# Convolution and a 16-expert layer on one core: narrower channel rows, ids alone in the token lists, and no GpSimd product

## The chip, the cores and the metric

The kernel runs on one core of a Trainium2 chip. The metric is the device time of one execution in microseconds (us). The kernel before takes 1279.42 us, the median of three runs (1278.69 to 1280.14). The engines are named as in the profile: PE (TensorE, matmuls and transposes), PEld (its weight loads), DVE (VectorE), ACT (ScalarE), POOL (GpSimd) and SP (SyncE, which issues most of the loads).

## The reference, cut to what matters

```python
# x: 8 x 2880 x 192; weight: 8 heads x 7 taps; N = 23040 tokens, D = 192, 4 x 4 experts, F = 1024
w = softmax(weight, axis=-1)
x = causal_conv(x, w)                  # per head of 24 channels, 7 taps, zeros ahead of each sequence
g_sm = softmax(x @ w_group);           g_idx = argmax(x @ w_group)
e_sm = softmax(x @ w_expert[g_idx]);   e_idx = argmax(x @ w_expert[g_idx])
out  = g_sm[g_idx] * e_sm[e_idx] * (relu(x @ w1[g_idx, e_idx]) @ w2[g_idx, e_idx])
```

Each token is sent to one expert of 16, and its result is scaled by the product of the two probabilities, its weight.

## The kernel before, in words

**Routing.** Tokens are handled in blocks of 120. A unit is a group of blocks: three units of 4, 8 and 12, three of 8, 8 and 8, then 12 each, 18 units (u0 to u17) in all. For each unit the input `xin` is loaded by SP; for each of 8 heads one matmul with a banded matrix makes the convolution (L419), and ACT copies it from PSUM into the unit's channel tile `xc` (L428). Rows of `xc` have XW = 256 columns: the 192 channels stand in columns 64 to 255, and ACT copies the last 64 of them once more into columns 0 to 63 (L431). ACT then issues the write of the whole tile to `xcd` in DRAM (L436), where the experts' stage finds a token's row by its id. `xc` rotates over 2 buffers (the pool `pa2`), so unit u+2's first copy needs unit u's write to be over.

Router logits need more than one pass of precision: the tile is transposed (L446, and L462 or L470) and split into a rounded part and a rest (ACT L449, L465, L471; DVE L450, L466, L472). From u8 on the last 64 channels of two blocks are transposed together, 128 columns at once (L462, "packed"); this needs two split steps on ACT and on DVE. Earlier units transpose block by block (L470). Three matmuls (L483) and transposes back (L495) give the logits; DVE and ACT make softmax and argmax (L531 to L562).

**Lists.** A unit's tokens get a position in the list of their expert. DVE writes two one-hot tables for six blocks at a time: `ohl` (L608) and `ohr` (L612, one buffer). POOL multiplies `ohr` by five bf16 columns `vals` (the low and high part of the id, and the weight in three bf16 pieces, L562 to L565) into `lts` (L616), and one matmul per block adds these up in PSUM (L631, 5 x 32 = 160 columns). ACT copies the result out (L637), DVE puts ids and weights together (L638 to L643), and POOL scatters them into the table `idtab` in DRAM, two columns (L645).

**Experts.** The work is a plan of slots of 256 tokens. Portion 0 has one slot for each of 16 experts and starts once u0 to u4 are listed; portion 1 has two per expert (needs u0 to u11) and portion 2 two more (needs all 18); the tail, nine items of 256 and nine of 128 tokens, is laid out at run time by DVE (`table`) from the counts. For a slot POOL gathers rows from `xcd` (L711, two gathers, into `xg` with 3 buffers), PE transposes them (L724, L726, or packed, L724 and L728, in portions 1 and 2), ACT and DVE split them (L729 to L741), and PE runs the first layer (`ph`, L752), whose output ACT (L757) and DVE (L758) turn into `hh` and `hl`, and then the second (`po`, L770 and L774). `finish` scales by the weight, read from the second column of the ids (ACT L821, DVE L822, tile `ys`), and POOL scatters the rows to the output (L825). Small tail items go through L787 to L813. An expert's weights come in five loads on SP (L660 to L664) into `raw` (6 buffers, a set needs 4) and are split by ACT and DVE (L676 to L692; in the tail POOL takes one of the splits, L685).

**What sets the order.** Each engine works through its own list in order. A generator per unit is stepped (`step`), and during the slots `advance` steps it between blocks of matmuls at a rate that has the units ready in time for the next portion; a tile scheduler then orders each engine's list by priorities. So list and routing steps of u5 to u17 lie between the matmuls of portions 0 and 1, while in portion 2 only expert work is left.

**The end.** Two loops stand behind the plan, each with a trip count read at run time: one (L1198) rebuilds the lists if an expert's share of one unit is too large, one (L1237) takes tail items beyond the 18. With these inputs both run zero times.

## Time and profile before

| | us |
|---|---|
| median of 3 runs | 1279.42 |
| the profiled execution | 1276.92 |
| its span, first to last instruction | 1275.2 |
| PE busy | 1132.9 (89%) |
| DVE busy | 907.9 (71%) |
| ACT busy | 721.9 (57%) |
| POOL busy | 554.1 (43%) |

The profiled execution stands 2.5 us under the median of the runs. PE's busy time counts matmuls only; the difference of it to the span, 142 us, is time in which PE ran none. The mean granted clock of PE is 0.941. Stages by the clock of the trace, from the span's start: until 155 us routing alone, 155 to 350 portion 0 with routing, 350 to 740 portion 1 with routing, 740 to 1101 portion 2, from 1101 the tail, whose last matmul ends at 1254.

### The profile page before, as it was taken

The page shows a single profiled execution, that of the slowest core. Times are in us where ns is not written, and L with a number is a line of the kernel's source. Part 1 is how long each engine was busy: PE and PEld are TensorE (multiplying, and loading weights), DVE is VectorE, ACT ScalarE, POOL GpSimd, SP SyncE. Part 2 cuts the span into 40 slices and gives each one's busy share as a digit, 9 for nine tenths or more (in the row PEclk, how much of TensorE's full clock was granted, in tenths as well). Part 3 has the DMA queues.
Part 4 walks back from the last instruction along what each step waited for, and adds up shares of the span by engine and source line. Part 5 has one row for each costly group of instructions (what it writes and reads, how often), then busy time and mean ns, then how long its engine had stood idle before and what let it go on. Part 6 is the DMA issues. An engine that isn't in the chain of part 4 may idle for free.

```text
span 1275.2 us, 23501 instructions
## 1 busy us (share of the span) xinstructions
PE 1132.9 (89%) x8080; PEld 1079.8 (85%) x8080; DVE 907.9 (71%) x2053; ACT 721.9 (57%) x1474; POOL 554.1 (43%) x473
## 2 busy tenths in 40 slices
PE   4677588888979999899989899999999999989993
PEld 3555487878979989898989899999999999988893
DVE  4777588898878767778677766666666665677771
ACT  4544256566756656455555355555555555677771
POOL 2121534333443443434444534444444444666751
PEclk8878688899989999899989989999999999999997
DMA  8955435777887747354454456454454544588860
GB/s 191 285 161 169 127 98 173 209 214 194 222 217 186 223 109 211 91 174 113 123 146 114 101 105 181 142 154 137 143 147 134 150 137 140 160 238 249 244 194 11
DMA packets 171740, 207.71 MB, mean 163 GB/s; under 512 B 27095, under 2 KB 145739, under 8 KB 171614
## 3 DMA queue, kind: packets, MB, share of 16 engines
q1 hardware_dynamic: 129566, 140.62, 41.0%
q0 software_dynamic: 18720, 41.93, 11.2%
q10 hardware_dynamic: 23328, 23.60, 6.0%
q8 instruction: 64, 1.05, 0.4%
q14 instruction: 62, 0.51, 0.1%
HBM read 164.92 MB, written 42.78 MB: 163 GB/s over the span
## 4 chain that ended last, share of the span: by engine, by line
PE 55%; DVE 16%; DMA 10%; issue 8%; ACT 5%; POOL 4%; SPq 1%; POOLq 0%; ACTq 0%; DVEq 0%
PE ph L752 23%; PE po L770 15%; PE po L774 7%; DMA raw<-in_moe_w 4%; POOL lts L616 3%; PE pm L419 3%; DVE hl L758 3%; DVE cw L692 2%; DMA out<-ys,idpt 2%; ACT cw L691 2%; PE pm L483 1%; PE pm L631 1%; ACT ys L821 1%; DVE tb L466 1%; DMA xcd<-xc 1%
## 5 line engine op out<-in xcount | busy, mean ns | idle before, releaser
L770 PE MATMUL po<-cw,hh 128*128 128x384 f32 x1424 | 450.7, 373 | 24.9 <-DVE ys L822 23.9
L752 PE MATMUL ph<-xa,ah 128*128 128x256 f32 x1424 | 393.6, 298 | 5.5 <-DVE hl L758 5.5
L774 PE MATMUL po<-cw,hl 128*128 128x192 f32 x1424 | 360.3, 253 | 0.0
L758 DVE SCALAR_TENSOR_TENSOR hl<-ph,hh 128x512 fp32r<-128x512 f32 x356 | 241.7, 686 | 130.2 <-ACT hh L757 124.6
L711 POOL DMA_INDIRECT xg<-xcd,idp x160 | 168.9, 1056 | 357.4 <-PE pm L728 214.2
L757 ACT ACTIVATE hh<-ph 128x512 fp32r<-128x512 f32 x356 | 209.1, 596 | 180.3 <-PE ph L752 173.7
L770 PEld LDWEIGHTS po<-cw,hh 128*128 128x128 f32 x1424 | 272.9, 192 | 30.8 <-DVE ys L822 26.8
L752 PEld LDWEIGHTS ph<-xa,ah 128*128 128x128 f32 x1424 | 276.2, 194 | 9.1 <-DVE hl L758 6.1
L774 PEld LDWEIGHTS po<-cw,hl 128*128 128x128 f32 x1424 | 276.9, 194 | 2.1
L825 POOL DMA_INDIRECT out<-ys,idp x160 | 187.2, 1170 | 120.7 <-DVE ys L822 82.3
L752 PE MATMUL ph<-xb,bh 128*128 128x256 f32 x712 | 204.4, 287 | 0.0
L752 PE MATMUL ph<-xb,bl 128*128 128x256 f32 x712 | 204.2, 287 | 0.0
L752 PE MATMUL ph<-xa,al 128*128 128x256 f32 x712 | 203.9, 286 | 0.0
L692 DVE TENSOR_TENSOR cw<-raw,cw 128x768 fp32r<-128x768 f32 x132 | 132.7, 1032 | 13.9 <-ACT cw L691 12.7
L752 PEld LDWEIGHTS ph<-xa,al 128*128 128x128 f32 x712 | 139.1, 195 | 1.8
L752 PEld LDWEIGHTS ph<-xb,bl 128*128 128x128 f32 x712 | 139.5, 196 | 0.0
L752 PEld LDWEIGHTS ph<-xb,bh 128*128 128x128 f32 x712 | 138.7, 195 | 0.0
L677 DVE TENSOR_TENSOR al<-raw,ah 128x1024 fp32r<-128x1024 f32 x66 | 82.8, 1255 | 36.3 <-ACT ah L676 23.5
L616 POOL TENSOR_TENSOR lts<-ohr,vals 120x960 bf16<-120x960 bf16 (+2 forms) x35 | 66.3, 1893 | 97.2 <-DVE ohr L612 49.3
L691 ACT ACTIVATE cw<-raw 128x768 fp32r<-128x768 f32 x132 | 105.4, 841 | 0.1
L736 ACT ACTIVATE xb<-pm 64x128 fp32r<-64x128 f32 x128 | 34.7, 271 | 92.3 <-DVE xa L730 44.2
L676 ACT ACTIVATE ah<-raw 128x1024 fp32r<-128x1024 f32 x66 | 70.0, 1060 | 27.8 <-DMA raw<-in_moe_w 11.8
(252 smaller groups left out, 1688.8 us busy)
## 6 DMA issues: line engine op xcount, KB each, us to landing
raw<-in_moe_w SPq DMA_DIRECT2D x132, 384.0 KB
raw<-in_moe_w SPq DMA_DIRECT2D x66, 512.0 KB
raw<-in_moe_w SPq DMA_DIRECT2D x132, 256.0 KB
xcd<-xc ACTq DMA_DIRECT2D x13, 1440.0 KB
xin<-in_x SPq DMA_DIRECT2D x7, 1134.0 KB
xin<-in_x SPq DMA_DIRECT2D x6, 1039.5 KB
xcd<-xc ACTq DMA_DIRECT2D x4, 960.0 KB
xg<-xcd,idp POOLq DMA_INDIRECT x160
```

Of the source, the lines that this page charges most:

```text
L616: OHE.tensor_tensor(out=ohv5[0:Q, 0:n], in0=ohr[0:Q, 0:n].unsqueeze(2).broadcast_to([Q, n, NV, LH]), in1=bc(vu[0:Q, bs], LH), op=ALU.mult,)
L676: pin(PINA, nc.scalar.activation(out=ah, in_=ra, func=AF.Copy))
L677: eng.get(k, nc.vector).tensor_tensor(out=al, in0=ra, in1=ah.bitcast(F32), op=ALU.subtract)
L691: pin(PINW, nc.scalar.activation(out=cw[:, fs, 0, :], in_=rc[k - 2], func=AF.Copy))
L692: eng.get(k, nc.vector).tensor_tensor(out=cw[:, fs, 1, :], in0=rc[k - 2], in1=cw[:, fs, 0, :].bitcast(F32), op=ALU.subtract,)
L711: nc.gpsimd.indirect_dma_start(out=xs[:, t, :], out_offset=None, in_=xcd[0:known, :], in_offset=bass.IndirectOffsetOnAxis(ap=ids[:, t, 0:1 ...
L752: nc.tensor.matmul(out=hp[:, j], lhsT=wgt[:, fs], rhs=xx, start=i == 0, stop=i == len(ops) - 1)
L757: nc.scalar.activation(out=hh, in_=hp, func=AF.Relu)
L758: nc.vector.scalar_tensor_tensor(out=hl, in0=hp, scalar=0.0, in1=hh.bitcast(F32), op0=ALU.max, op1=ALU.subtract,)
L770: nc.tensor.matmul(out=oo[t][:, 0:2 * D], lhsT=hh[:, j, ts], rhs=cw[:, f].rearrange("p a d -> p (a d)"), start=f == 0, stop=False,)
L774: nc.tensor.matmul(out=oo[t][:, 0:D], lhsT=hl[:, j, ts], rhs=cw[:, f, 0, :], start=False, stop=f == NF - 1,)
L825: nc.gpsimd.indirect_dma_start(out=outviews[nscat[0] % len(outviews)], out_offset=bass.IndirectOffsetOnAxis(ap=ids[:, t, 0:1].bitcast(U32) ...
```

## The change

- Rows of `xc`, `xcd` and `xg` have 193 columns (XW = D + 1): 192 channels, then the token's weight. The copy into the doubled columns (L431) goes. `reciprocal` writes the weight straight into column 192 of `xc`, and the write to `xcd` moves behind it, from the end of the convolution to the end of the softmax; it is still issued by ACT, the whole unit at once. `xc` gets a third buffer.
- `vals` has two columns (the id). The five DVE steps on the weight (L562 to L565) and two on the lists (L642, L643) go. The product with `ohr` moves from POOL to DVE, has a tile `ohv` of its own, and makes 6 x 2 x 32 = 384 columns instead of 960; the list matmul has 64 columns instead of 160. `idtab` has one column.
- Packed transposes go, in the router (from u8 on two more transposes per quarter unit of four blocks, one split step less on ACT and on DVE) and in the slots of portions 1 and 2 (four transposes instead of three, one split step less on ACT and on DVE).
- `finish` reads the weight from the gathered row. `xg` gets a fourth buffer.
- Weights: `raw` and `rawc`, three buffers each, instead of six `raw`; in the tail the loads of a set are issued up to three slots further ahead, every second set into `xin` and `xc` tiles, which are free by then.
- The two loops at the end are nested in an outer loop, whose flag the table's code works out, so that one loop is skipped instead of two. `LISTLAG0` is 0 and changes nothing.

The core of the diff:

```diff
-NV = 5
+NV = 2
-    RAWB = 6
+    RAWB = 3
-    XW = D + D2
+    XW = D + 1
-    idtab = dram.tile([ROWS, 2], I32, name="idtab")
+    idtab = dram.tile([ROWS, 1], I32, name="idtab")
-    OHE = nc.gpsimd
+    OHE = nc.vector
-    NXG = 3
+    NXG = 4
...
-        xc = pa2.tile([P, UB, XW], F32, name="xc")
+        xc = pa2.tile([P, UB, XW], F32, name="xc", bufs=3)
...
-            dup.tensor_copy(out=xc[0:BT, 0:nb, 0:D2], in_=xc[0:BT, 0:nb, D:XW])
-        xcw = xcd[t0:t0 + nb * BT, :].rearrange("(b p) d -> p b d", p=BT)
-        for q in range(0, nb, SQ):
-            SE.dma_start(out=xcw[:, q:q + min(SQ, nb - q)], in_=xc[0:BT, q:q + min(SQ, nb - q)])
...
-            if PACKU[0] <= u < PACKU[1]:
...
             for i in range(QB):
-                nc.tensor.transpose(psb[0:D2, i * BT:(i + 1) * BT], xc[0:BT, q * QB + i, D:XW], ident[0:BT, 0:BT])
+                nc.tensor.transpose(psb[0:D2, i * BT:(i + 1) * BT], xc[0:BT, q * QB + i, P:D], ident[0:BT, 0:BT])
...
-        nc.vector.reciprocal(out=se, in_=se)
-        nc.vector.tensor_copy(out=vu[0:Q, :, 2], in_=se)
-        for k in (3, 4):
-            nc.vector.tensor_tensor(out=se, in0=se, in1=vu[0:Q, :, k - 1], op=ALU.subtract)
-            nc.vector.tensor_copy(out=vu[0:Q, :, k], in_=se)
+        nc.vector.reciprocal(out=xc[0:Q, 0:nb, D], in_=se)
+        xcw = xcd[t0:t0 + nb * BT, :].rearrange("(b p) d -> p b d", p=BT)
+        SE.dma_start(out=xcw, in_=xc[0:BT, 0:nb])
...
-            ohv5 = pa.tile([P, 512], F32, name="lts", bufs=2).bitcast(BF16)[:, 0:HB2 * NV * LH].rearrange(
-                "p (b v r) -> p b v r", b=HB2, v=NV)
+            ohv5 = pa.tile([P, HB2, NV, LH], BF16, name="ohv", bufs=2)
...
-        nc.vector.tensor_tensor(out=lv5[:, 2], in0=lv5[:, 2], in1=lv5[:, 3], op=ALU.add)
-        nc.vector.tensor_tensor(out=lsi.bitcast(F32)[:, :, 1], in0=lv5[:, 2], in1=lv5[:, 4], op=ALU.add)
...
+        if spare:
+            rab = pa2.tile([P, UB, D], F32, name="xin").rearrange("p b d -> p (b d)")
+            ra, rb = (rab[:, k * F:(k + 1) * F] for k in range(2))
+            rcc = pa2.tile([P, UB, XW], F32, name="xc", bufs=3).rearrange("p b d -> p (b d)")
...
+            nc.tensor.transpose(px[:, t * P:(t + 1) * P], xs[:, t, 0:P], ident)
+            nc.tensor.transpose(px[0:D2, SLOT + t * P:SLOT + (t + 1) * P], xs[:, t, P:D], ident)
...
-            g = ids.bitcast(F32)[:, t, 1:2]
+            g = xs[:, t, D:XW]
...
+    def tail_weights(i, take=True):
+        if tail0 <= i < len(plan) and i not in tailw:
+            j = plan[i][1]
+            tailw[i] = weights(
+                *tail_regs(lambda c: tab[0][0:1, j, c:c + 1], 2), {1: nc.gpsimd}, spare=(i - tail0) % 2 == 0)
+        return tailw[i] if take else None
...
+        for q in range(i + 1, i + 1 + TAHEAD):
+            if tab[0] is not None and len(units) == routed[1]:
+                tail_weights(q, False)
...
-    with tc.For_i(0, nover, 1):
+    with tc.For_i(0, nrare[0], 1):
...
+        with tc.For_i(0, nover, 1):
...
+        with tc.For_i(NTAIL, nend[0], 1) as i:
```

How the order of each engine's list moves is shown at three places. The first is ACT's list in the routing stage, before, where the tile of a unit with 8 blocks is written (L436); `tb` is a split step, and the wait names in brackets are the semaphores of DMA queues (DMAHW) and engines.

```order
79 L431 ACTIVATE xc<-xc 120x8x64 [waits Activation_49]
80 L436 DMA xcd<-xc 120x8x256 [waits DMAHW3_49,Activation_49]
81 L471 ACTIVATE tb<-po 64x480 [waits PE_49]
82 L428 ACTIVATE xc<-ph 120x8x24 [waits DMAHW4_49,PE_49]
83 L471 ACTIVATE tb<-ph 64x480 [waits PE_49]
```

The same engine in the changed kernel, where a unit of 8 blocks is written (L536) and three rows further on the first convolution copy (L423, L428 before) into the next buffer waits on a DMA.

```order
73 L444 ACTIVATE tb<-po 64x480 [waits PE_49,Activation_49]
74 L536 DMA xcd<-xc 120x8x193 [waits DVE_49]
75 L461 ACTIVATE lts<-ph 120x480 [waits PE_49]
76 L444 ACTIVATE tb<-ph 64x480 [waits PE_49,Activation_49]
77 L423 ACTIVATE xc<-ph 120x8x24 [waits DMAHW0_49]
78 L423 ACTIVATE xc<-po 120x8x24
```

In both a copy into `xc` stands some three rows behind a write. Before, with two buffers, the write that the copy waits for is that of two units earlier; in the changed kernel, with three buffers and the write moved behind the softmax, it is that of three units earlier, and this is the write that stands just ahead of it.

The second place is DVE's list around the lists of a unit in portion 1, before (`hl` belongs to the hidden layer, `xa` and `xb` to the transposed rows of the next slot, `ys` to the output of the last one).

```order
831 L608 TENSOR_TENSOR ohl<-iop,posb 120x768
832 L612 TENSOR_TENSOR ohr<-ior,posb 120x192
833 L608 TENSOR_TENSOR ohl<-iop,posb 120x768
834 L466 TENSOR_TENSOR tb<-pm,tb 64x2x120
835 L612 TENSOR_TENSOR ohr<-ior,posb 120x192
836 L758 SCALAR_TENSOR_TENSOR hl<-ph,hh 128x512
837 L730 TENSOR_TENSOR xa<-pm,xa 128x256
838 L822 SCALAR_TENSOR_TENSOR ys<-po,idp_1167,ys 128x192
```

And in the changed kernel, with the products `ohv` (L586) on DVE:

```order
750 L578 TENSOR_TENSOR ohl<-iop,posb 120x768
751 L582 TENSOR_TENSOR ohr<-ior,posb 120x192
752 L578 TENSOR_TENSOR ohl<-iop,posb 120x768
753 L586 TENSOR_TENSOR ohv<-ohr,vals 120x384
754 L722 SCALAR_TENSOR_TENSOR hl<-ph,hh 128x512
755 L582 TENSOR_TENSOR ohr<-ior,posb 120x192
756 L701 TENSOR_TENSOR xa<-pm,xa 128x256
757 L586 TENSOR_TENSOR ohv<-ohr,vals 120x384
758 L786 SCALAR_TENSOR_TENSOR ys<-po,xg_197,ys 128x192
```

Two products have come in and a split step has left; the first `ys` still stands behind both `ohr`, and now behind both products too.

The third place is the end of ACT's list before, where the last `ys` stands behind the first loop's branch.

```order
1181 L821 ACTIVATE ys<-po,idpt 128x192 x2
1182 L798 ACTIVATE hh<-pm 128x512
1183 L1197 TENSOR_LOAD over
1184 L1198 COMPARE_AND_BRANCH
1185 L1198 UNCONDITIONAL_BRANCH x2
1186 L1274 BRANCH_PREFETCH_HINT
1187 L1198 REGISTER_ALU
1188 L1198 COMPARE_AND_BRANCH
1189 L1198 UNCONDITIONAL_BRANCH
1190 L821 ACTIVATE ys<-po,idpt 128x192
```

In the changed kernel the last `ys` (L785) stands ahead of the one outer branch (L1189).

```order
1121 L785 ACTIVATE ys<-po,xg_197 128x192 x2
1122 L762 ACTIVATE hh<-pm 128x512
1123 L785 ACTIVATE ys<-po,xg_198 128x192
1124 L1139 TENSOR_LOAD flagi
1125 L1189 COMPARE_AND_BRANCH
```

The last output step has moved ahead of the skip on ACT; the scatter that it feeds, on POOL, stands behind the loop in both kernels.

More of the change, by code (lines that the diff above doesn't have):

```diff
@@ L236, in conv_moe_kernel @@
     LIM = SLOT * sum(spe for _, spe in portions)
-    fill = const.tile([P, 2 * LIM // P], I32, name="fill")
+    fill = const.tile([P, LIM // P], I32, name="fill")
     nc.gpsimd.memset(fill, BIG)
@@ L445, in turn_a @@
             for i in range(QB):
-                nc.tensor.transpose(psa[:, i * BT:(i + 1) * BT], xc[0:BT, q * QB + i, D2:D], ident[0:BT, 0:BT])
+                nc.tensor.transpose(psa[:, i * BT:(i + 1) * BT], xc[0:BT, q * QB + i, 0:P], ident[0:BT, 0:BT])
             tah = pa.tile([P, QN], F32R, name="tah", bufs=QS)
@@ L625, in unit @@
         nc.vector.tensor_tensor(out=rowi, in0=rows[:, E:E + 1], in1=goff, op=ALU.add)
-        for _ in range(LISTLAG if u >= NEED else 0):
+        for _ in range(LISTLAG if u >= NEED else LISTLAG0 if u < NEED - 1 else 0):
             yield
@@ L836, in close_table @@
         yield
-        seen = const.tile([P, 2, 2], I32, name="seen")
+        seen = const.tile([P, 2, 1], I32, name="seen")
         nc.sync.dma_start(
-            out=seen, in_=TABV[0:2, :].unsqueeze(0).broadcast_to([P, 2, 2]))
+            out=seen, in_=TABV[0:2, :].unsqueeze(0).broadcast_to([P, 2, 1]))
         nc.vector.tensor_scalar(out=seen, in0=seen, scalar1=0, scalar2=BIG, op0=ALU.bitwise_and, op1=ALU.bitwise_or)
@@ L852, in close_table @@
                 yield
+    flags = const.tile([P, 2], F32, name="flags")
+    flagi = const.tile([P, 2], I32, name="flagi")
     def table(first=None, nbig=NBIG, nsmall=NSMALL):
@@ L891, in table @@
         tt(t["rem"], endr, base, ALU.subtract)
+        if first is None:
+            ts(flags[:, 0:1], most, float(SLOT), ALU.is_gt)
+            ts(flags[:, 1:2], most, float(SLOT), ALU.is_le)
+            ts(t["rem"], t["rem"], flags[:, 1:2], ALU.mult)
         slots(t["nf"], P - 1 if first is None else SLOT - 1)
@@ L934, in table @@
         v.tensor_copy(out=enti, in_=ent)
+        if first is None:
+            ts(flags[:, 1:2], ent[:, 3:4], float(NTAIL), ALU.is_gt)
+            tt(flags[:, 1:2], flags[:, 0:1], flags[:, 1:2], ALU.max)
+            v.tensor_copy(out=flagi, in_=flags)
         yield
@@ L1016, in open_tail @@
             yield
-        idps["tail"] = const.tile([P, NTAIL, 2, 2], I32, name="idpt")
+        idps["tail"] = const.tile([P, NTAIL, 2, 1], I32, name="idpt")
         for j in range(NTAIL):
@@ L1028, in open_portion @@
         rows = spe * 2
-        idp = const.tile([P, E, rows, 2], I32, name=f"idp{pi}")
+        idp = const.tile([P, E, rows, 1], I32, name=f"idp{pi}")
         if pi == 0:
@@ L1094, in open_slot @@
         if pi == "tail":
-            W = weights(*tail_regs(lambda c: tab[0][0:1, e, c:c + 1], 2), {1: nc.gpsimd})
+            W = tail_weights(i)
             ids = idps["tail"][:, e]
@@ L1162, in conv_moe_kernel, with fold @@
                 hr = hidden_small(W, turned[i], f2)
-                def fold(W=W, oo=oo, hr=hr, f2=f2, ids=ids, last=last):
+                def fold(W=W, oo=oo, hr=hr, f2=f2, ids=ids, xs=gathered[i], last=last):
                     HH = turn_small(hr)
@@ L1169, in fold2 @@
                         if last:
-                            finish(oo, ids)
+                            finish(oo, ids, xs)
                     later(LAG_S, fold2)
```

190 lines of the change are left out of this document (80 added, 110 removed).

## The prediction

> **What bounds the kernel now.** I read the page first, then busy time by stage, the waits, and the chain of work that ended last in the stages that wait. Of the page two rows matter: PE's share, and the product that the change takes from POOL (busy, mean ns, idle before it).
>
> ```profile
> PE 1132.9 (89%) x8080; PEld 1079.8 (85%) x8080; DVE 907.9 (71%) x2053; ACT 721.9 (57%) x1474; POOL 554.1 (43%) x473
> ...
> L616 POOL TENSOR_TENSOR lts<-ohr,vals 120x960 bf16<-120x960 bf16 (+2 forms) x35 | 66.3, 1893 | 97.2 <-DVE ohr L612 49.3
> ```
>
> PE is the bound, but not everywhere. The windows by stage show where (length, then busy time of PE, PEld, DVE, ACT and POOL with instructions, then the granted clock, the DMA share and GB/s):
>
> ```profile
> 0.00:155.00 155.00, 95.05 (x467) 71.95 (x467) 104.98 (x414) 69.62 (x171) 43.62 (x57) 0.79 0.68 188
> 155.00:350.00 195.00, 173.59 (x1182) 162.56 (x1182) 167.38 (x399) 121.04 (x247) 77.68 (x60) 0.92 0.66 184
> 350.00:740.00 390.00, 359.29 (x2632) 348.99 (x2631) 289.56 (x670) 215.36 (x450) 169.55 (x143) 0.96 0.55 151
> 740.00:1101.00 361.00, 361.00 (x2792) 361.00 (x2792) 232.74 (x406) 203.95 (x407) 167.22 (x150) 1.00 0.50 142
> 1101.00:1254.00 153.00, 143.81 (x1014) 135.29 (x1012) 112.82 (x167) 111.52 (x201) 94.90 (x64) 1.00 0.76 213
> ```
>
> PE stands for 60 us in the routing stage, 21 in portion 0, 31 in portion 1, not at all in portion 2, and 9 in the tail. A gain can come from those sums and from the clock that falls with them; in portion 2 any added PE instruction is added time. The waits of the stages (us in total, times, longest), first those of the routing stage, then one of portion 0, then one of portion 1:
>
> ```profile
> PE pm L631 <- POOL lts L616: 23.7, 8, 7.0
> POOL xg L711 <- issue: 17.3, 9, 14.8
> ACT xc L428 <- DMA xcd<-xc: 3.6, 1, 3.6
> ```
>
> ```profile
> PE pm L631 <- POOL lts L616: 16.1, 7, 3.9
> ```
>
> ```profile
> PE po L770 <- DVE ys L822: 23.9, 10, 6.1
> ```
>
> So the list matmul's wait for POOL's product is two fifths of PE's stand in the routing stage (23.7 of 60) and most of it in portion 0 (16.1 of 21). In portion 1 it is not that wait: there PE waits for DVE.
>
> **Routing stage, first half: the product leaves POOL.** Near its end the chain of waits shows what the product queues behind (start us, us, what):
>
> ```profile
> 29.61 13.89 DMA xcd<-xc
> ...
> 111.57 14.60 issue
> 126.39 0.35 POOL xg L711
> ...
> 134.03 1.81 POOL lts L616
> ...
> 149.28 1.81 POOL lts L616
> ```
>
> From 111.57 to 126.39 POOL stands before a gather that needs ids, then come six gathers, and only at 134.03 the product of a list that DVE had ready. On DVE it queues behind no gather. What it costs there no row shows; the nearest are the two one-hot steps on DVE (busy us, mean ns):
>
> ```profile
> L608 DVE TENSOR_TENSOR ohl<-iop,posb 120x768 bf16<-120x768 f32 x30 | 28.6, 953 | 0.3
> ...
> L612 DVE TENSOR_TENSOR ohr<-ior,posb 120x192 bf16<-120x192 f32 x30 | 10.6, 354 | 15.8 <-POOL lts L616 15.8
> ```
>
> 192 elements take 354 ns and 768 take 953, so 384 would take 354 + 192 x 599/576 = 0.55 us; the two rows are the bounds. Eight waits of 0.55 us remain of the 23.7: a gain of 19 us. The bounds are 0, if the time to slot 0 is set by gathers and ids anyway, and the whole 24.
>
> **Second half: the write to xcd moves behind the softmax.** This is the change's new wait. The write is issued by ACT, and a few rows on stands the first copy of the unit that takes the same buffer; it waits for the landing. Behind it on ACT wait all PSUM copies, split steps and lists, and PE needs their banks. The distance in ACT's list is this short for five units, u4 to u8; later ones have slot work between. The nearest rows are the 13.89 us of a write on the chain (with issue and queue) and the 3.6 us that ACT stood at the same kind of wait before. I take the second, since ACT is busy for 69.62 of 155 us and most of a landing lies in time in which it waits for PE anyway: 5 x 3.6 = 18 us of ACT, of which a good half, 10 us, shows on PE. The ends are 0 and 5 x 13.89 = 69. The stage's sum is **-19 + 10 = -9**. The copy of the doubled columns (L431) goes at zero, as ACT is not the bound here.
>
> [...]
>
> **Portion 0.** One unit's list in the timeline (start us, us, engine, line, idle before and its releaser), and the clock in the windows of 2 us behind it:
>
> ```profile
> 209.84 0.35 DVE L612 TENSOR_TENSOR ohr<-ior,posb 120x192 bf16<-120x192 f32 x1
> ...
> 210.27 2.43 POOL L616 TENSOR_TENSOR lts<-ohr,vals 120x960 bf16<-120x960 bf16 x1 [2.29 <-DVE ohr L612]
> 212.74 0.36 DVE L612 TENSOR_TENSOR ohr<-ior,posb 120x192 bf16<-120x192 f32 x1 [1.23 <-POOL lts L616]
> 212.76 0.57 PE L631 MATMUL pm<-lts,ohl 120*128 120x160 bf16 x6 [3.15 <-POOL lts L616]
> ...
> 213.25 1.80 POOL L616 TENSOR_TENSOR lts<-ohr,vals 120x960 bf16<-120x960 bf16 x1 [0.54 <-DVE ohr L612]
> ...
> 215.09 0.96 PE L631 MATMUL pm<-lts,ohl 120*128 120x160 bf16 x6 [1.25 <-POOL lts L616]
> ```
>
> ```profile
> 214.00:216.00 2.00, 0.91 (x7) 0.90 (x7) 2.00 (x2) 0.00 (x1) 1.84 (x2) 0.50 0.00 0
> ...
> 218.00:220.00 2.00, 2.00 (x10) 1.59 (x8) 1.42 (x2) 1.84 (x3) 1.62 (x2) 0.50 0.74 242
> ```
>
> PE stands from 209.6 (212.76 - 3.15). After the change the second `ohl` ends at about 211.05, the first product at 211.6, `ohr` and the second product at 212.5: PE's 4.4 us (3.15 + 1.25) become some 2.3, or 48% less. Of the 16.1 us that is **-7.7**. The clock stands at 0.50 from 214 for 6 us and more, which costs 3 us and somewhat, say 3.4. Four units are listed here; I let the shorter gap keep the clock in two: **-6.8**. Bounds: 0 (all four keep the half clock) and -13.6.
>
> [...]
>
> **Portion 1.** The largest of the ten waits on `ys`:
>
> ```profile
> 375.07 2.44 POOL L616 TENSOR_TENSOR lts<-ohr,vals 120x960 bf16<-120x960 bf16 x1 [6.17 <-DVE ohr L612]
> ...
> 377.54 0.36 DVE L612 TENSOR_TENSOR ohr<-ior,posb 120x192 bf16<-120x192 f32 x1 [1.25 <-POOL lts L616]
> ...
> 379.33 0.69 PE L770 MATMUL po<-cw,hh 128*128 128x384 f32 x1 [6.12 <-DVE ys L822]
> ```
>
> Of PE's 6.12 us only 1.25 is DVE waiting for POOL; the rest is DVE's own list ahead of `ys`. The change takes away the 1.25 and puts two products there, 1.1 us. So this stage's wait does not go, it changes its name. About 0.3 us for each of seven units: **-2**, between -10 (if each wait gets short enough for the clock) and +5 (if a product takes the 0.95 of the upper row).
>
> **Transposes.** Two rows from the timeline show pairs:
>
> ```profile
> 399.83 0.38 PE L724 MATMUL pm<-ident,xg 128*128 128x128 f32 x2
> ```
>
> ```profile
> 196.16 0.37 PE L462 MATMUL pm<-ident,xc 120*128 120x120 f32 x2
> ```
>
> One alone lasts about 0.27, so the second adds 0.11 and 0.10. One more in each of 64 slots of portions 1 and 2 is 7.0 us, two more in each of 30 quarters of u8 to u17 is 60 x 0.103 = 6.2: **+13.2**, of which portion 2's 32 slots, with no idle time on PE, pay theirs in full. The split steps that go on ACT and DVE are counted at nothing. The narrower list matmul (64 columns for 160): six took 0.57 us, one alone about 0.28, so 0.06 each, 192 in all, but the weight load stays: **-2**, between 0 and -7.
>
> **Tail and end.** In the tail the chain passes through a weights landing for each pair of items, 17 us apart, and the waits there name one short one of PE (8 times):
>
> ```profile
> 1161.38 5.71 DMA raw<-in_moe_w
> ...
> 1178.33 6.18 DMA raw<-in_moe_w
> ```
>
> ```profile
> PE po L813 <- DVE hl L799: 7.7, 8, 1.1
> ```
>
> PE stands for only 9.2 us there, and earlier weights don't touch the handing over at L813. I take **-4**, between 0 and -9. What the longer look-ahead could cost is SP time in portion 2, where the DMA share is 0.50.
>
> Behind the last matmul the profile shows two skips in series. The rows of the last output step and scatter, and of the second skip on POOL:
>
> ```profile
> 1258.96 0.42 ACT L821 ACTIVATE ys<-po,idpt 128x192 f32<-128x192 f32 x1 [6.57 <-issue]
> ...
> 1266.49 0.98 POOL L825 DMA_INDIRECT out<-ys,idpt  x1 [12.36 <-issue]
> ```
>
> ```profile
> L1234 POOLq TENSOR_LOAD <-tab x1: 307/307/307, 1261.8 to 1261.8; - x1
> ```
>
> ```profile
> L1237 POOLq COMPARE_BRANCH  x3: 32/33/45, 1262.2 to 1265.5; - x3
> ...
> L1237 POOLq INC_SWDGE_SEM  x1: 1821/1821/1821, 1262.5 to 1262.5; - x1
> ```
>
> On POOL the second skip runs from its flag's load at 1261.8 to its last branch at 1265.5, 3.7 us, and 3.9 with the step to the next instruction; with the loops nested it is not reached. **-3.9**, between -3 and -6. The scatter behind it stays.
>
> **The sum.** -9 (routing) - 7.7 - 6.8 (portion 0) - 2 (portion 1) - 2 (list matmuls) + 13.2 (transposes) - 4 (tail) - 3.9 (end) = -22.2. From the profiled execution's 1276.92 that gives 1254.7. The median of the runs stands 2.5 us above that execution, so the forecast is 1257.
>
> **The rivals.** First, slower: the write's landing takes over. If each of the five copies waits not 3.6 but about 10 us, all on PE, the routing stage gets 50 instead of 10 us: +40, 1297. It decides from 33 us on (22.2 + the 10 in the sum = 32.2 for no change), that is 6.5 per unit. For it speak the 13.89 us row and ACT's list in order; against it, that the same wait cost 3.6 before, and that ACT has nothing to do for over half of this stage. Chance 0.12.
>
> Second, the gain is halved: slot 0 waits for its ids and gathers whoever makes the product (routing 0 instead of -9), and the clock still falls at each list in portion 0 (6.8 back): 1257 + 15.8 = 1273. For it speaks that the 14.60 us on the chain is a wait for ids, not for the product. Chance 0.20.
>
> [...] Chance 0.12.
>
> Fourth, the change does little: if a transpose on a busy PE cost its 0.27 us, the 124 would cost 33 instead of 13.2: 1257 + 20 = 1277. The pairs' rows speak against it. Chance 0.06.
>
> **How the numbers follow.** The forecast itself has 0.50. A difference of 0.2%, 2.6 us, is about what the measurement can tell. Faster by more: the forecast, the second and the third rival, 0.82; within it 0.05, most of the fourth; slower 0.13, the first rival and a little of the others' upper ends. The range reaches from the full gain, 1234, to 1284, where the write's stall is 37 us: some 0.1 lies above, and some 0.08 below.
>
> **What would show it.** Right: first expert matmul (155.28 before) some 9 us earlier; PE's wait at the list matmul in portion 0 halved and named after DVE; the waits for `ys` in portion 1 as they were; portion 2 longer by 3.5 us; one skip at the end. Wrong: a wait of ACT at its convolution copies for the write of more than 33 us in all, or a routing stage as long as before.

## The result and the profile after

The changed kernel takes 1227.0 us (median of 4 runs, 1225.0 to 1232.9); the kernel before, run beside it, 1279.1. The ratio is 0.961 (95% interval 0.956 to 0.965). The forecast was right in direction and 30 us too long, and its range, from 1234, does not hold the result: the gain is 52 us where 22 was summed up.

The profiled execution takes 1228.73 us with a span of 1226.8, against 1275.2. To compare work with work and not clock time with clock time, I cut both traces at the same four matmuls: the first of the experts' first layer, the first of portion 1, the first of portion 2 and the first of the tail (numbers 1, 641, 1921 and 3201 of 3560), and at the end of the last matmul. The windows of the kernel before between these points (length, busy PE, PEld, DVE, ACT, POOL, then granted clock, DMA share, GB/s); portions 0 and 1:

```profile
143.10:407.80 264.70, 227.95 (x1565) 213.83 (x1565) 221.87 (x522) 158.03 (x320) 109.03 (x86) 0.91 0.69 190
407.80:789.60 381.80, 359.75 (x2653) 351.23 (x2652) 274.59 (x633) 208.75 (x440) 169.04 (x144) 0.96 0.52 142
```

And of the changed kernel, from routing to the end:

```profile
0.00:133.90 133.90, 84.50 (x439) 63.01 (x439) 93.07 (x350) 59.73 (x156) 22.50 (x41) 0.83 0.68 164
133.90:377.70 243.80, 219.79 (x1603) 206.20 (x1601) 209.35 (x469) 147.80 (x294) 77.11 (x68) 0.96 0.76 194
377.70:747.50 369.80, 354.97 (x2708) 347.19 (x2707) 264.59 (x568) 200.85 (x392) 152.30 (x133) 0.99 0.56 141
747.50:1060.60 313.10, 313.10 (x2434) 313.10 (x2433) 199.70 (x320) 176.38 (x321) 135.66 (x130) 1.00 0.48 137
1060.60:1210.20 149.60, 145.83 (x1030) 136.89 (x1028) 114.58 (x168) 112.59 (x203) 106.43 (x69) 1.00 0.77 209
1210.20:1226.80 16.60, 0.00 (x0) 0.00 (x0) 0.42 (x1) 0.42 (x1) 0.97 (x1) 0.65 0.04 11
```

Beside the prediction's terms, sorted by stage (the transposes are 2.5 us in portion 0, 7.2 in portion 1 and 3.5 in portion 2; the list matmuls 1 each in portions 0 and 1), the stages read:

| stage | before | after | difference | forecast |
|---|---|---|---|---|
| routing, to the first expert matmul | 143.1 | 133.9 | -9.2 | -9.0 |
| portion 0 | 264.7 | 243.8 | -20.9 | -13.0 |
| portion 1 | 381.8 | 369.8 | -12.0 | +4.2 |
| portion 2 | 309.4 | 313.1 | +3.7 | +3.5 |
| tail, to the last matmul | 155.2 | 149.6 | -5.6 | -4.0 |
| end | 21.0 | 16.6 | -4.4 | -3.9 |

At these cuts four of six stages came out within 2 us, and portions 0 and 1 make 24 of the 26 us that the sum missed, portion 1 alone 16. But the first cut is not the one that the prediction meant. It put the first expert matmul at 155.28; that is the eleventh, where a long run of them starts. The first one starts at 143.12, and between the ninth and the tenth PE stands at a list matmul. Cut at the eleventh, routing went from 155.3 to 140.2, which is -15.1, and portion 0 from 252.5 to 237.5, which is -15.0. So how the 30 us fall to these two stages hangs on the cut; portion 1 does not. The two windows of the routing stage at this cut, before and after:

```profile
0.00:155.30 155.30, 95.35 (x467) 72.25 (x468) 105.25 (x416) 69.62 (x171) 43.62 (x57) 0.79 0.68 188
```

```profile
0.00:140.20 140.20, 87.70 (x467) 65.48 (x468) 98.59 (x369) 61.50 (x160) 24.68 (x43) 0.84 0.68 164
```

In portion 1 the rows say where the gain is: PE stood for 22.0 us before and 14.8 after. The clock is the other half. By the clock records of the traces PE ran for 24 us at half clock before and for 7 after, which costs 12.1 and 3.4 us by the estimate that work takes twice as long then; in the trace of before successive transposes of `xc` (L446) start 200 ns apart at half clock and 102 at full, matmuls of the first layer 213 and 120. (The clock of the windows times their length, 0.96 of 381.8 and 0.99 of 369.8, gives more, 15.3 and 3.7: it is rounded, and counts half clock under which PE stands.) The two make -16; PE's own work, with more transposes and narrower list matmuls, grew by 4 us, and -12.0 is left. Stand and clock have about equal shares.

The waits of the changed kernel, first the two in the whole span that answer to those shown of before, then ACT's new one:

```profile
PE pm L601 <- DVE ohv L586: 24.0, 13, 4.9
...
ACT xc L423 <- DMA xcd<-xc: 21.6, 6, 6.2
...
PE po L734 <- DVE ys L786: 12.8, 9, 4.7
```

The list matmul waited 39.8 us for POOL's product and waits 24.0 for DVE's. The wait for `ys`, which was to stay, fell from 23.9 us to 12.8. ACT's wait for the late write is 21.6 us in six waits, where 18 in five was forecast.

### The profile page after: what moved, and what is told of

The parts are those of the page before. It is cut to its first block, busy times and chain, and to the rows that moved or that the text cites. A ratio compares the mean times of both kernels' runs of the same rounds, so it can differ in the third digit from the quotient of the medians.

```text
span 1226.8 us, 23625 instructions
## 1 busy us (share of the span) xinstructions
PE 1118.2 (91%) x8204; PEld 1066.4 (87%) x8204; DVE 881.7 (72%) x1872; ACT 697.8 (57%) x1362; POOL 495.0 (40%) x439
## 4 chain that ended last, share of the span: by engine, by line
PE 58%; DVE 13%; DMA 7%; issue 5%; ACT 3%; POOL 1%; SPq 1%; POOLq 0%; DVEq 0%; ACTq 0%
PE ph L716 26%; PE po L734 16%; PE po L738 7%; DVE hl L722 3%; PE pm L414 2%; DMA xg<-xcd,idpt 2%; DMA out<-ys,idpt 2%; PE pm L456 2%; DVE ohl L578 1%; DVE cw L666 1%; DMA raw<-in_moe_w 1%; PE pm L698 1%; PE pm L699 1%; DMA xg<-xcd,idp 1%; DVE tb L445 1%
## 5 line engine op out<-in xcount | busy, mean ns | idle before, releaser
L734 PE MATMUL po<-cw,hh 128*128 128x384 f32 x1424 | 445.8, 371 | 13.0 <-DVE ys L786 12.8
L716 PE MATMUL ph<-xa,ah 128*128 128x256 f32 x1424 | 389.3, 295 | 4.8 <-DVE hl L722 4.8
L789 POOL DMA_INDIRECT out<-ys,idp x160 | 166.6, 1041 | 479.7 <-DVE ys L786 424.3
L734 PEld LDWEIGHTS po<-cw,hh 128*128 128x128 f32 x1424 | 269.5, 189 | 18.1 <-DVE ys L786 14.8
L685 POOL DMA_INDIRECT xg<-xcd,idp x160 | 189.2, 1183 | 59.3 <-issue 29.9
L666 DVE TENSOR_TENSOR cw<-rawc,cw 128x768 fp32r<-128x768 f32 x114 | 105.5, 954 | 15.5 <-ACT cw L665 14.1
L704 ACT ACTIVATE xb<-pm 64x256 fp32r<-64x256 f32 x98 | 36.0, 368 | 109.6 <-DVE xa L701 109.6
L786 DVE SCALAR_TENSOR_TENSOR ys<-po,xg,ys 128x192 f32<-128x192 f32 x187 | 76.3, 416 | 23.8 <-ACT ys L785 16.7
L665 ACT ACTIVATE cw<-rawc 128x768 fp32r<-128x768 f32 x114 | 91.0, 837 | 1.4 <-DMA rawc<-in_moe_w 1.4
L651 DVE TENSOR_TENSOR al<-raw,ah 128x1024 fp32r<-128x1024 f32 x57 | 70.4, 1234 | 28.7 <-ACT ah L650 28.1
L785 ACT ACTIVATE ys<-po,xg 128x192 f32<-128x192 f32 x187 | 76.5, 419 | 22.0 <-PE po L738 10.7
```

Of the source, the lines that this page charges most:

```text
L651: eng.get(k, nc.vector).tensor_tensor(out=al, in0=ra, in1=ah.bitcast(F32), op=ALU.subtract)
L665: pin(PINW, nc.scalar.activation(out=cw[:, fs, 0, :], in_=rc[k - 2], func=AF.Copy))
L666: eng.get(k, nc.vector).tensor_tensor(out=cw[:, fs, 1, :], in0=rc[k - 2], in1=cw[:, fs, 0, :].bitcast(F32), op=ALU.subtract,)
L685: nc.gpsimd.indirect_dma_start(out=xs[:, t, :], out_offset=None, in_=xcd[0:known, :], in_offset=bass.IndirectOffsetOnAxis(ap=ids[:, t, 0:1 ...
L716: nc.tensor.matmul(out=hp[:, j], lhsT=wgt[:, fs], rhs=xx, start=i == 0, stop=i == len(ops) - 1)
L734: nc.tensor.matmul(out=oo[t][:, 0:2 * D], lhsT=hh[:, j, ts], rhs=cw[:, f].rearrange("p a d -> p (a d)"), start=f == 0, stop=False,)
```

## The experiments

In the comparisons below each run stands against the kernel before on the same chip; the stages are cut as above, from one profiled execution each. Run 6 changes the tail alone, and its routing stage is 2.3 us longer than the changed kernel's (136.2 and 133.9), so a few us there are no evidence.

| run | us | ratio (interval) | routing | portion 0 | portion 1 | portion 2 | tail | end |
|---|---|---|---|---|---|---|---|---|
| before | | 1 | 143.1 | 264.7 | 381.8 | 309.4 | 155.2 | 21.0 |
| changed | 1227.0 | 0.961 (0.956-0.965) | 133.9 | 243.8 | 369.8 | 313.1 | 149.6 | 16.6 |
| 1 product on POOL | 1244.3 | 0.974 (0.971-0.978) | 147.4 | 249.7 | 367.8 | 313.9 | 149.2 | 16.6 |
| 2 large product on DVE | 1254.2 | 0.983 (0.980-0.986) | 137.7 | 257.5 | 374.1 | 309.4 | 152.3 | 21.4 |
| 3 unpacked | 1276.1 | 1.000 (0.998-1.002) | 149.5 | 265.1 | 374.5 | 313.0 | 153.3 | 20.9 |
| 4 early write | 1207.5 | 0.947 (0.944-0.951) | 120.4 | 237.9 | 365.2 | 313.1 | 149.7 | 16.7 |
| 5 split write | 1223.9 | 0.959 (0.955-0.962) | 131.1 | 244.4 | 367.9 | 313.4 | 149.3 | 16.7 |
| 6 no look-ahead | 1262.8 | 0.989 (0.985-0.992) | 136.2 | 244.4 | 366.2 | 313.1 | 186.1 | 17.0 |
| 7 unread POOL product | 1283.5 | 1.005 (1.001-1.008) | 141.8 | 270.2 | 388.9 | 313.7 | 148.2 | 17.0 |
| 8 large product on DVE, unpacked | 1254.5 | 0.981 (0.977-0.986) | 139.3 | 255.2 | 369.5 | 313.0 | 155.1 | 21.2 |
| 9 split write, later | 1220.6 | 0.957 (0.953-0.961) | 129.6 | 251.7 | 367.9 | 313.1 | 148.3 | 16.7 |
| 10 split write by SP | 1210.5 | 0.951 (0.948-0.955) | 120.7 | 242.4 | 366.2 | 313.3 | 148.9 | 16.6 |
| 11 old weights, two xc buffers | 1275.6 | 1.001 (0.998-1.004) | 174.6 | 248.0 | 366.9 | 313.2 | 154.7 | 16.8 |

My theory after the result was that the missed gain lies on DVE: POOL's product had held up DVE's list ahead of `ys` and of the list matmul more than its wait row shows (theory A). The rivals were that only the product's size matters (B), and that it is the split steps that went with the packing (C).

**Run 1**, one part undone.

```diff
-    OHE = nc.vector
+    OHE = nc.gpsimd
```

> The changed kernel (1227.0), with its product of 384 columns back on GpSimd. Theory A (the engine matters: VectorE waits for GpSimd's product and is held up beside it, and the product queues behind gathers): the routing stage loses some 9 us, portions 0 and 1 together some 10, so 1240 to 1250, and the waits at the list matmul are named after POOL again. Theory B (the size matters, a product of 384 columns is short wherever it runs): within 5 us of the changed kernel, 1227 to 1232.

It took 1244.3, 17 us of the gain gone, as A said, but not where A said. Portion 1 is no longer than in the changed kernel (367.8), portion 0 is by 6, and 13.5 us are in the routing stage. There POOL's timeline shows eight gathers and then the product (first, last and product: start us, us, idle before), and PE's longest wait at a list matmul of that stage is 10.9 us where the changed kernel has 4.9:

```profile
124.00 1.04 POOL L685 DMA_INDIRECT xg<-xcd,idp  x1 [11.84 <-DMA idp<-idtab]
...
133.46 1.01 POOL L685 DMA_INDIRECT xg<-xcd,idp  x1 [0.30 <-issue]
134.49 0.84 POOL L586 TENSOR_TENSOR ohv<-ohr,vals 120x384 bf16<-120x384 bf16 x1
```

So in the routing stage the queue on POOL counts, as forecast. In portion 1 a product of 384 columns, 1.04 us in the mean of the run, costs nothing on either engine: there theory B is right: by this run the smaller product alone would have done for that stage.

**Run 2**, that part alone, in the kernel before.

```diff
-    OHE = nc.gpsimd
+    OHE = nc.vector
```

> The kernel before (1279), with its product of 960 columns on VectorE and nothing else. On VectorE it should take about 1.15 us (354 ns + 768 x 1.04). Theory A: most of the gain of routing, portion 0 and portion 1 is there with this alone, 1240 to 1255. Theory B: VectorE's list grows by 2.3 us a unit ahead of ys, portion 1 gets no shorter or longer, and the whole stays at 1265 to 1280.

1254.2: over two fifths of the gain (1.7% of 3.9%) with one word, spread over routing (-5.4), portion 0 (-7.2) and portion 1 (-7.7). The product took 1.15 us there, as estimated (and the one of 384 columns 0.55, as the prediction had it):

```profile
L616 DVE TENSOR_TENSOR lts<-ohr,vals 120x960 bf16<-120x960 bf16 x30 | 34.6, 1152 | 0.0
```

In portion 1 this adds 2.3 us a unit to DVE's list, and the stage is still shorter. By the prediction's account, DVE gets 1.25 us back and pays 2.3, and the stage should have been longer. The trace of before has one thing more that POOL's products took from DVE in portion 1, besides 6.1 us of waits: steps that ran beside them were 2.2 us longer than usual. That makes 8.3 us, and the products that came onto DVE take 11.5, so this sum does not explain the gain. The order of DVE's list differs in places too (the copy `eold` stands ahead of `xa` at 520.9 before, behind it at 510.4 here); what that is worth was not taken apart.

**Run 3**, another part alone, in the kernel before.

```diff
-    PACKU = (8, 99)
-    PACKS = (1, 2)
+    PACKU = (99, 99)
+    PACKS = ()
```

> The kernel before (1279), with the packed transposes of units and slots unpacked and nothing else: 124 more transposes on TensorE, one split step less on ScalarE and VectorE for each slot and quarter. By the prediction's term it is 13 us longer, 1292. Theory C (the steps that go on VectorE are what shortens the waits for ys in portion 1): the wait falls by some 10 us, and the time stays at 1275 to 1284; portion 2 is longer by 3.5 us in either case.

1276.1, no difference to the kernel before where the transposes alone say +13. Portion 2, where PE is always busy, pays its 3.6 us. Portion 1 is 7.3 us shorter although it has 7.2 us more of transposes at the prediction's price: by that price the split steps that went give back some 14 us there. The wait for `ys` in portion 1, of the kernel before and of this run:

```profile
PE po L770 <- DVE ys L822: 17.8, 9, 3.5
```

```profile
PE po L770 <- DVE ys L822: 12.0, 7, 2.4
```

The longest falls from 3.5 to 2.4 us, and all of PE's stand in portion 1 from 22.0 to 13.7. The clock of the window is 0.98 instead of 0.96; by the clock records half clock cost PE's running time 12.1 us before and 8.3 here. So C holds too, beside what run 2 shows. The run takes the split steps from ACT as well as from DVE, and that it is DVE's alone that count is not shown.

```profile
414.60:789.10 374.50, 360.79 (x2709) 353.55 (x2707) 268.71 (x589) 204.43 (x396) 167.03 (x144) 0.98 0.52 144
```

**Run 8**, both together.

```diff
-    OHE = nc.gpsimd
+    OHE = nc.vector
-    PACKU = (8, 99)
-    PACKS = (1, 2)
+    PACKU = (99, 99)
+    PACKS = ()
```

> The kernel before (1277) with both: the product of 960 columns on VectorE, and all transposes unpacked. Alone the first gave -23 and the second 0. If they help the same queue on VectorE, portion 1 gains less than the sum of both (7.6 and 7.2 us), and the time is 1254 to 1262; if they add up, 1250 to 1254.

1254.5, where the two ranges meet, so the total does not decide. Portion 1 is 12.3 us shorter, the whole of what it gained in the changed kernel (12.0) and less than the two alone (7.7 + 7.3), as if both shortened one queue; with one profiled execution each, 2.7 us are thin evidence for that. Portion 0 is 9.5 us shorter, of 20.9: the rest of that stage's gain is neither the engine alone nor the packing.

**Run 7**, the cost of standing beside it: the changed kernel with a product on POOL whose result nobody reads.

```diff
+            nc.gpsimd.tensor_tensor(
+                out=dum[0:Q, 0:n], in0=ohl[0:Q, 0:n, 0:LH].unsqueeze(2).broadcast_to([Q, n, 5, LH]),
+                in1=bc(ohl[0:Q, 0:n, LH:LH + 5], LH), op=ALU.mult,
+            )
```

> The changed kernel (1227.0) with one GpSimd product of 960 columns for each half unit added, made of the one-hot table ohl, whose result nobody reads. If GpSimd's product holds up VectorE's steps that read only the on-chip memory (up to 1.1 us each, as in the trace of before), routing and the two portions are longer by 4 to 12 us in all, 1231 to 1239, and some cw or al step of VectorE takes 1.5 us or more. Rival: only the wait for its result cost, and the time stays within 2 us.

1283.5, longer by 56 us, with the result read by nobody: nearly five times the upper end that I had given it. Portion 0 has 26 us more, portion 1 has 19. Not all of it is DVE's: the product's tile shares its two buffers with ACT's copies of the logits, which waited for it,

```profile
ACT lts L461 <- POOL lts L592: 12.0, 4, 4.5
```

and it also keeps POOL from what stands behind it, 60.7 us for the 30 products of full size. So 56 us is an upper bound of what DVE's standing costs. What the trace gives for DVE itself is 46 us by which its steps beside the product were longer than their median (10.9 in routing, 20.4 in portion 0, 14.5 in portion 1). DVE's timeline around one unit's lists, and POOL's beside it:

```profile
521.30 0.35 DVE L582 TENSOR_TENSOR ohr<-ior,posb 120x192 bf16<-120x192 f32 x1
...
523.02 0.65 DVE L445 TENSOR_TENSOR tb<-pm,tb 64x480 fp32r<-64x480 f32 x1
523.70 4.02 DVE L582 TENSOR_TENSOR ohr<-ior,posb 120x192 bf16<-120x192 f32 x1
527.65 0.68 DVE L728 SCALAR_TENSOR_TENSOR hl<-ph,hh 128x512 fp32r<-128x512 f32 x1
```

```profile
523.94 3.56 POOL L592 TENSOR_TENSOR lts<-ohl 120x960 bf16<-120x960 bf16 x2
```

The step that takes 0.35 us at 521.30 takes 4.02 at 523.70, and ends when two POOL products in a row have ended. Behind it wait `hl` and `ys`, and behind these PE. In the whole run `ohr` takes 784 ns in the mean instead of 352, `ohv` 949 instead of 552, `ohl` 1332 instead of 954:

```profile
L578 DVE TENSOR_TENSOR ohl<-iop,posb 120x768 bf16<-120x768 f32 x30 | 40.0, 1332 | 0.5
L586 DVE TENSOR_TENSOR ohv<-ohr,vals 120x384 bf16<-120x384 bf16 x30 | 28.5, 949 | 0.1
L582 DVE TENSOR_TENSOR ohr<-ior,posb 120x192 bf16<-120x192 f32 x30 | 23.5, 784 | 0.1
```

The trace of before shows the same in small. There one of DVE's weight splits took 2.1 us, at 247.4 beside a product, with a median of 0.95. (The rows below give the least, the median and the greatest duration in ns.) The greatest alone misleads, though. Of the twelve splits over 1.2 us four run beside a product; the other eight are in the tail, beside POOL's own weight split, and the changed kernel has such steps as well, in the row of its tiles in `xc`:

```profile
L692 DVE TENSOR_TENSOR cw<-raw,cw x132: 944/953/2115, 32.6 to 1243.8; 128x768 fp32r<-128x768 f32 x132
```

```profile
L666 DVE TENSOR_TENSOR cw<-rawc,cw x114: 906/953/961, 35.2 to 1199.9; 128x768 fp32r<-128x768 f32 x114
L666 DVE TENSOR_TENSOR cw<-xc,cw x18: 943/956/1915, 1048.7 to 1194.7; 128x768 fp32r<-128x768 f32 x18
```

In all, DVE's steps beside POOL's products were 2.0 us too long in the routing stage of before, 6.1 in portion 0 and 2.2 in portion 1.

The steps named here that took longer beside a product, `ohr`, `ohv`, `ohl` and `cw`, have both inputs in SBUF; and at 523.70 `ohr` stood for two products, not for one.

**Run 4**, the new wait taken away.

```diff
+        nc.vector.memset(xc[0:BT, 0:nb, D], 1.0)
+        xcw = xcd[t0:t0 + nb * BT, :].rearrange("(b p) d -> p b d", p=BT)
+        SE.dma_start(out=xcw, in_=xc[0:BT, 0:nb])
         lg = rt.tile([P, UB, NL], F32, name="lg")[:, 0:nb]
...
-        nc.vector.reciprocal(out=xc[0:Q, 0:nb, D], in_=se)
-        xcw = xcd[t0:t0 + nb * BT, :].rearrange("(b p) d -> p b d", p=BT)
-        SE.dma_start(out=xcw, in_=xc[0:BT, 0:nb])
+        nc.vector.reciprocal(out=se, in_=se)
```

> The changed kernel (1227.0) with the write to xcd back at the end of the convolution, column 192 filled with ones ahead of it: the weights are left out, so the output is not scaled. It takes ScalarE's wait for the landing away (21.6 us in 6 waits). By the prediction's term TensorE gets 10 us back, 1217. Rival: slot 0 waits for its ids and gathers anyway, and less than 4 us is seen, 1223 to 1228.

1207.5: the late write costs 19.5 us by the medians and some 17 by the ratios, twice the term. Between the profiled executions it is 23.7 us, 13.5 of them in routing and 10.5 in the two portions behind. In the routing stage PE's waits for ACT's copies into `xc`, the price that the prediction put at 10 us, are 11.3 us in the changed kernel and 2.7 in this run.

**Run 5**, a complete kernel without the wait for the landing: the channels are written early, the weight alone late.

```diff
+        SE.dma_start(out=xcw[:, :, 0:D], in_=xc[0:BT, 0:nb, 0:D])
         lg = rt.tile([P, UB, NL], F32, name="lg")[:, 0:nb]
...
+        wcol = rt.tile([P, UB], F32, name="wcol")
+        nc.vector.reciprocal(out=wcol[0:Q, 0:nb], in_=se)
+        SE.dma_start(out=xcw[:, :, D:XW], in_=wcol[0:BT, 0:nb].unsqueeze(2))
```

> The changed kernel (1227.0) with the 192 channels written to xcd at the end of the convolution, as before, and the weight alone, from a small tile of its own, behind the softmax: complete output, and no copy of the next unit waits for the late write. The run with the weights left out took 1207.5. If the landing of the late write is what cost those 19.5 us, 1205 to 1212 here; if the 4-byte pieces of the second write are dear (1440 of them a unit, on the gathers' path), 1215 or more.

1223.9, only 3 us less. ACT waits for no landing now, and PE's waits for its copies are 2.9 us instead of 11.3, so that part of the cost is gone; something else has come. ACT stands for 6.4 us before the small write's issue, and it looks as if the issue, which waits for DVE's softmax, held the split step behind it. PE's and DVE's rows beside ACT's show what it waits for:

```profile
50.16 0.32 ACTq L425 DMA_DIRECT2D xcd<-xc  x1
55.55 0.97 PE L414 MATMUL po<-xin,band 126*120 126x192 f32 x2 [4.85 <-DMA xin<-in_x]
56.41 0.73 PE L458 MATMUL ph<-tah,wrz 128*120 128x480 f32 x1
56.61 0.17 DVE L551 TENSOR_TENSOR off<-ph,eoff 128x16 f32<-128x16 f32 x1 [3.74 <-PE ph L548]
56.93 0.32 ACTq L538 DMA_DIRECT2D xcd<-wcol  x1
57.30 0.57 ACT L437 ACTIVATE tah<-pm 128x480 fp32r<-128x480 f32 x1 [6.30 <-PE ph L458]
```

PE waits 4.85 us for an input load, DVE's list with the softmax's last step waits for PE, and ACT's split step is released by PE (L458) as well. At 67.1 PE waits for another load, 4.49 us. The changed kernel has no such wait in its routing stage.

**Run 10**, the same small write from SP, whose list holds mostly loads (the edit is against run 5).

```diff
-        SE.dma_start(out=xcw[:, :, D:XW], in_=wcol[0:BT, 0:nb].unsqueeze(2))
+        nc.sync.dma_start(out=xcw[:, :, D:XW], in_=wcol[0:BT, 0:nb].unsqueeze(2))
```

> As the run with the split write (1223.9), but the weight's small write is issued by SyncE behind the softmax. ScalarE waits for nothing, so 1206 to 1214 if ScalarE's standing was the cost; but the loads queued on SyncE behind each of these waits start later, and if these loads were what the routing stage waits for, 1218 or more.

1210.5, ratio 0.951 (0.948 to 0.955) to the kernel before: a complete kernel, faster than the kernel before and the changed one, and within 3 us of run 4 (5 by the ratios). Routing is 120.7 us, as in run 4, so the 4-byte pieces are not dear. Runs 5 and 10 differ in nothing but the queue that issues the small write, and that is 13 us by the medians, some 9 by the ratios, as the two were measured on different chips. The time fits the first range, but not for its reason: of the 10.4 us between the two routing stages 9.3 are PE's two waits for input loads in run 5, and here PE waits for none but once, 1.0 us at 15.9. SP itself stands 63.7 us in 13 waits before the small writes:

```profile
SPq L538 <- DVE wcol L537: 63.7, 13, 13.0
```

In run 5 SP issues loads of weights from 32.5 us on and the next input load at 41.5; here, where it stands before the small write until 36.0, these loads come at 36.3 and the input load at 38.1. That the times of the loads are the cause fits, but no run changes them alone.

**Run 9**, the small write still on ACT, but issued behind the unit's list steps (against run 5).

```diff
-        SE.dma_start(out=xcw[:, :, D:XW], in_=wcol[0:BT, 0:nb].unsqueeze(2))
...
+        SE.dma_start(out=xcw[:, :, D:XW], in_=wcol[0:BT, 0:nb].unsqueeze(2))
         pl = bank("l")
```

> As the run with the split write (1223.9), but the weight's small write is issued by ScalarE only behind the unit's list steps on VectorE, some stages later, so that ScalarE does not stand before it until the softmax is over (6.4 us at 50.5 in the split run). If that standing in order is what kept the split run from 1207.5, 1206 to 1214. Rival: the small write itself is late for slot 0's gathers or slow, and the time stays at 1220 to 1227.

1220.6, with runs from 1214.5 to 1229.0, in the rival's range. The profiled execution, the slowest of the four, speaks against ACT's standing before the issue as the cost. The split step is now ahead of the issue in ACT's list, and ACT stands for 6 us before it all the same, while PE waits for the same load:

```profile
54.70 0.96 PE L414 MATMUL po<-xin,band 126*120 126x192 f32 x2 [4.45 <-DMA xin<-in_x]
56.33 0.57 ACT L437 ACTIVATE tah<-pm 128x480 fp32r<-128x480 f32 x1 [6.00 <-PE ph L458]
56.39 0.32 ACTq L599 DMA_DIRECT2D xcd<-wcol  x1
```

Whether the small write makes the loads late when it goes through ACT's queue is open.

**Runs 6 and 11**, the tail's weights.

```diff
-    TAHEAD = 3
+    TAHEAD = 0
...
-    {1: nc.gpsimd}, spare=(i - tail0) % 2 == 0)
+    {1: nc.gpsimd}, spare=False)
```

> The changed kernel (1227.0) without the look-ahead of the tail's weights (each set loaded when its slot is opened, none into xin or xc). By the prediction's term the tail gives back 4 to 6 us, 1231 to 1233. Rival: the tail's gain comes from the gather's fourth buffer or from VectorE, and the time stays within 1.5 us.

1262.8, far outside both ranges: the tail took 186 us. With the new buffers the look-ahead, with the spare tiles that it loads into, is not worth 5 us but 36. Run 11 puts the old buffers back too.

```diff
-    RAWB = 3
+    RAWB = 6
-    TAHEAD = 3
+    TAHEAD = 0
...
-            ra, rb = (wraw.tile([P, F], F32, name="raw") for _ in range(2))
-            rc = [wraw.tile([P, HF, D], F32, name="rawc") for _ in range(2)]
+            raw = [wraw.tile([P, F], F32, name="raw") for _ in range(4)]
+            ra, rb = raw[0], raw[1]
+            rc = [r[:, 0:HF * D].rearrange("p (f d) -> p f d", d=D) for r in raw[2:]]
...
-        xc = pa2.tile([P, UB, XW], F32, name="xc", bufs=3)
+        xc = pa2.tile([P, UB, XW], F32, name="xc", bufs=2)
```

> The changed kernel (1227.0) with the weights as before the change: one set of six buffers, no look-ahead in the tail; to make room for them xc has two buffers instead of three. In the tail (from its first matmul to the last one) the prediction's term says 153 to 156 us, as before the change (155.2), against 149.5; the run without look-ahead but with the new buffers had 186. In the routing stage two buffers make the copies wait for the write of two units earlier, 10 us or more.

The tail is 154.7 us, as before the change (155.2), so buffers and look-ahead together gain 5 us. Why the new buffers alone lose 31 us was not tested; both arrangements hold a set and a half. In run 6's tail SP's longest waits are those of the `rawc` loads for DVE's last splits of the set before:

```profile
SPq L638 <- DVE cw L666: 82.8, 9, 11.2
```

The run's second half shows what the prediction's first rival describes: with two `xc` buffers ACT waits 51.6 us for the write in routing, and that stage is 40.7 us longer.

```profile
ACT xc L423 <- DMA xcd<-xc: 51.6, 6, 11.5
```

## Why the prediction was right or wrong

**Routing, near in the sum, and that by luck.** -19 + 10 = -9; measured are -9.2 at the first expert matmul and -15.1 at the one that the prediction meant. The write's +10 was right: PE's waits for ACT's copies into `xc` are 11.3 us, and ACT's 3.6 us for each landing came out exactly (21.6 in six). The -19 was not. Eight waits of 0.55 us were to remain of the 23.7; what remains is 13.6 in six, since the product now comes late in DVE's list:

```profile
PE pm L601 <- DVE ohv L586: 13.6, 6, 4.9
```

So the two terms together are about zero. The gain came from what the prediction did not count: by the two windows above PE's stand fell by 7.5 us, 6.4 of them waits for input loads that the changed kernel does not have, and PE's busy time fell by 7.6 us for the same number of instructions, with a clock of 0.84 instead of 0.79. Such waits are 6.4 to 15.9 us in the kernel before and in runs 2, 3 and 8, which are made from it, and none in runs 1, 6 and 7, made from the changed kernel; which part of the change takes them away was not tested.

**Portion 1, wrong: this is the step that failed.** "So this stage's wait does not go, it changes its name", and for the split steps, "counted at nothing". The prediction read from one timeline that DVE waits 1.25 us for POOL and pays 1.1 us for the products, and forecast +4.2 us for the stage with its transposes; -12.0 was measured. The wait did go in part: the waits for `ys` in portion 1 fell from 17.8 us to 10.7, PE's stand in all from 22.0 to 14.8. Two of the prediction's prices were wrong. A POOL product of 960 columns costs this stage more than the 1.25 us: without it on POOL the stage is 7.7 us shorter although DVE's list gets 2.3 us a unit longer (run 2), and a product of 384 columns costs nothing there on either engine (run 1). And the split steps are not worth nothing: run 3 gives back some 14 us for them. Together the two give the whole 12 us (run 8). How the product's price comes about is shown only in part: steps of DVE stand beside it (run 7), but that and the waits make 8.3 us in portion 1 of before, less than the 11.5 that run 2 adds to DVE. On top of it the clock was left out of this stage. It is 8.7 of the 16 us that the stage gained against PE's added work; PE's gaps of over 2 us went from six to two there, and the falls of the clock from five to two.

**Portion 0, right.** At the prediction's own cut -15.0 for -13. PE's stand fell by 9.2 us there, for -7.7: its wait at the list matmul went from 16.1 to 10.4 us, not quite halved, and is named after DVE. The clock gave 7.6 us, for -6.8, though not as forecast. It was to be kept at two of four lists, a choice of mine that no row of before showed; by the clock records it fell at three before (at 214.0, 244.7 and 282.2, for 6.8 us each) and at three after (at 194.6, 225.4 and 286.8), but for 3.4 us each. At the cut of the table the stage gained 20.9; of these, run 8 shows 9.5 for the engine and the unpacking; the smaller product, the narrower list matmul and the steps on `vals` were not taken apart. The list matmul was undervalued: six take 0.35 us instead of 0.57, so 7 us for all 192 and not 2.

```profile
192.16 0.35 PE L601 MATMUL pm<-ohv,ohl 120*128 120x64 bf16 x6 [1.32 <-DVE ohv L586]
```

**Transposes, right on PE and wrong in the sum.** Portion 2 pays 3.7 us (3.5 forecast); where PE also waits, what they cost came back through the split steps that go with them (run 3).

**Tail and end, right.** -5.6 and -4.4, for -4 and -3.9. PE's stand in the tail fell from 9.2 to 3.8 us, as the term had it. That the new buffers by themselves lose 31 us and the look-ahead gains 36 was not foreseen.

**The rivals.** The first, the late write, had the right mechanism: it decides with two buffers (run 11, +40.7 in routing) and takes 17 to 19.5 us with three. The second is refuted in its first half by run 1, where the product's queue behind the gathers makes the routing stage 13.5 us longer; of its second half it is true that the clock still falls, at three lists, but for half as long. The third, the full gain at 1234, was the nearest, and run 10 went past it; it had the clock kept at all four lists, 6.8 us that no run shows: after the change it falls at three, for 3.4 us each. The fourth is refuted by portion 2.

## What to carry to other kernels

When two engines share a queue of small steps, read not only the wait rows but each step's least, median and greatest duration: a step that now and then takes twice its median (`cw` before, 2.1 us for 0.95) may be standing beside another engine, and no wait row tells of it; look at what runs beside each long one. Before you put a stand down to the instruction that ends it, find a run in which that instruction stands elsewhere: run 9 has the same stand as run 5 (6.0 and 6.3 us). Put the cuts between stages at points that mean the same in both traces, and try a second cut before you call a stage's forecast right. And where gaps of one to three microseconds repeat, count the clock that they cost beside the gaps themselves (in portion 1 it gave 8.7 us, the gaps 7.2).
